# A fixed instruction order on every engine, and zero-padded keys for full-array scores, in a retention plus feed-forward kernel

## The chip, the cores and the metric

The kernel runs on one core of one Trainium2 chip. The time is device microseconds per execution, the median of several runs. Engines are called PE (matmul; PEld its weight loads), DVE (VectorE), ACT (ScalarE), POOL (GpSimd) and SP (SyncE, which issues the transfers). The "chain" of a profile is the work that ended last, followed back from the last instruction. In these kernels PE writes its results into buffers in PSUM, and ACT or DVE copies them out again ("evicts"; in the kernel before, `qkT<-T` on ACT took 1.01 us and `xT<-O` on DVE 0.69 us). Tile names in the profiles: qn and kn are the scaled queries and keys, T their transposes, qT, kpad or qkT the evicted ones, sc the scores, R the masked scores, vpad the padded values, O the output, st the state, xT the attention's result, ph and po the up- and down-projection.

## The reference, cut to what matters

```python
def _attn_ref(q, k, v):                        # 8 batches, 8 heads, 576 tokens, 64 dims
    scores = scale * np.matmul(q, k.transpose(0, 1, 3, 2))
    gamma = 1.0 - 2.0 ** (-5.0 - np.arange(H))
    Dmat = np.where(rel >= 0, gamma[:, None, None] ** rel[None], 0.0)   # decay, causal
    return np.matmul(scores * Dmat, v)
def _moe_ref(x, w_in, w_out, beta):            # x: 4608 x 512, w_in: 512 x 2048
    h = x @ w_in
    return (h * (1.0 / (1.0 + np.exp(-beta * h)))) @ w_out
```

There is no softmax, so the attention of a batch is done in five chunks of tokens (four of 128 and one of 64) with a running state: a chunk needs its own 128 x 128 scores, and the earlier chunks enter through the state.

## The kernel before

Per chunk: scale q and v by the decay, transpose q and k on PE into one PSUM bank `T`, evict with one ACT copy, scores, causal mask on DVE, output, state. `HP` is 4, pairs of heads; two heads share a 128-row tile, so the scores of one head contract over 64 rows only.

```python
        qkT = sb.tile([P, 2, HP, P], BF16, name="qkT", tag="qkT", bufs=3)
        nc.scalar.copy(qkT[:, :, :, :cL], T[:, :, :, :cL])
        ...
        with tc.manual_schedule(engines={PE}):          # order fixed inside this block only
            for p in range(HP):
                for j in range(2):
                    r = slice(j * D, (j + 1) * D)       # rows 0-63 or 64-127: half the array
                    nc.tensor.matmul(sc[j][:cL, p, :cL], qkT[r, 1, p, :cL], qkT[r, 0, p, :cL], ...)
        for j in range(2):
            nc.vector.tensor_tensor(R[:cL, j, :, :cL], sc[j][:cL, :, :cL], m_b, ALU.mult)
    ...
    for b in range(1, B + 1):                           # a scheduler orders what this emits
        if b < B:
            for c in range(NC):
                load_chunk(b, c)
                if b == 1 and c == NC - 1:
                    load_w_out()                        # after all loads of batch 1
            for c in range(NC):
                attn_chunk(b, c)
        moe_up(b - 1, range(FO))                        # 64 matmuls 128x512, 16 Silu on ACT
        moe_down(b - 1)                                 # 64 matmuls 128x512
```

Of the kernel before, what the change touches and what calls it, by code (L numbers as in the profile page):

```python
# [11 lines left out]
F32 = mybir.dt.float32  # L12
# [7 lines left out]
def kernel(  # L20
# [10 lines left out]
    nc = tc.nc  # L31
# [21 lines left out]

    qkv_tiles = {}

    def load_chunk(b, c):
        c0, cL = chunks[c]
        t = stage.tile([P, 3, H, D], F32, name="qkvn", tag="qkvn", bufs=7)
        for i, src in enumerate((q, k, v)):
            nc.sync.dma_start(t[:cL, i], src[b, :, c0:c0 + cL, :].rearrange("h s d -> s h d"))  # L60
        qkv_tiles[(b, c)] = t

    for c in range(NC):
        load_chunk(0, c)
# [3 lines left out]

    ident_f = consts.tile([P, P], F32, name="ident_f")
# [8 lines left out]
    pos = consts.tile([P, NC], F32, name="pos")  # L78
    nc.gpsimd.iota(pos[:], pattern=[[P, NC]], base=0, channel_multiplier=1,
                   allow_small_or_imprecise_dtypes=True)  # L80
    lg = consts.tile([P, NC, H], F32, name="lg")
    for h in range(H):
        nc.vector.tensor_scalar(lg[:, :, h], pos[:], math.log(1.0 - 2.0 ** (-5.0 - h)), None, ALU.mult)
    gq = consts.tile([P, NC, H], F32, name="gq")
    gv = consts.tile([P, NC, H], F32, name="gv")
    nc.scalar.activation(gq[:], lg[:], ACT.Exp)
    nc.scalar.activation(gv[:], lg[:], ACT.Exp, scale=-1.0)
    nc.vector.tensor_scalar(gq[:], gq[:], scale, None, ALU.mult)


    NV = 3
    vpads = []
    for i in range(NV):
        vp = consts.tile([P, H, P], BF16, name=f"vpad{i}")
        nc.gpsimd.memset(vp[:], 0.0)
        vpads.append(vp)

    NS = 2
    sbds = []
    for i in range(NS):  # L100
        s = consts.tile([P, HP, P], BF16, name=f"sbd{i}")
        nc.gpsimd.memset(s[:], 0.0)
        sbds.append(s)
# [6 lines left out]
    pb = psum.tile([P, FO], F32, name="pb", tag="T", bufs=1)  # L110
    nc.tensor.transpose(pb[:], beta_rows[:], ident_f[:FO, :FO])

    tiny = consts.tile([P, FO], F32, name="tiny")
    nc.vector.tensor_copy(beta_sb[:], pb[:])
    nc.vector.tensor_tensor(tiny[:], beta_sb[:], beta_sb[:], ALU.mult)
    nc.vector.tensor_scalar(tiny[:], tiny[:], 1e-24, 1e-12, ALU.is_lt, ALU.mult)
    nc.vector.tensor_tensor(beta_sb[:], beta_sb[:], tiny[:], ALU.add)
    nc.vector.reciprocal(rbeta_sb[:], beta_sb[:])

# [3 lines left out]
    w_out_r = moe_w_out.rearrange("(fo fi) n -> fi fo n", fi=P)  # L123
    for g in range(WG):
        t = stage.tile([P, KO, FG], F32, name="wt", tag="wt", bufs=3)
        nc.sync.dma_start(t[:], w_in_r[:, :, g * FG:(g + 1) * FG])
        nc.vector.tensor_copy(w_in_sb[:, :, g * FG:(g + 1) * FG], t[:])  # L127

    def load_w_out():
        for g in range(WG):  # L130
            t = stage.tile([P, KO, d_model], F32, name="wt", tag="wt", bufs=3)
            nc.sync.dma_start(t[:], w_out_r[:, g * KO:(g + 1) * KO, :])
            for i in range(KO):
                fo = g * KO + i
                nc.vector.tensor_scalar(w_out_sb[:, fo, :], t[:, i], rbeta_sb[:, fo:fo + 1], None, ALU.mult)  # L135
# [4 lines left out]
    cnt = [0]  # L140

    def attn_chunk(b, c):
        c0, cL = chunks[c]
        t = qkv_tiles.pop((b, c))
        first = b == 0
        qn = sb.tile([P, H, D], BF16, name="qn", tag="qn", bufs=2)
        kn = sb.tile([P, H, D], BF16, name="kn", tag="kn", bufs=3)
        vp = vpads[cnt[0] % NV]
# [4 lines left out]
        eq = nc.vector if first else nc.gpsimd  # L153
        eq.tensor_tensor(qn[:cL], t[:cL, 0], gq_b, ALU.mult)  # L154
        if first:
            nc.scalar.copy(kn[:cL], t[:cL, 1])
        else:
            nc.gpsimd.tensor_copy(kn[:cL], t[:cL, 1])  # L158
        nc.gpsimd.tensor_tensor(vp4[:cL], t[:cL, 2].rearrange("p (pr two) d -> p pr two d", two=2),  # L159
                                gv_b.rearrange("p (pr two) d -> p pr two d", two=2), ALU.mult)  # L160

        T = psum.tile([P, 2, HP, P], BF16, name="T", tag="T", bufs=1)
        for i, src in enumerate((qn, kn)):
            for p in range(HP):
                nc.tensor.transpose(T[:, i, p, :cL],  # L165
                                    src[:cL, 2 * p:2 * p + 2, :].rearrange("p h d -> p (h d)"),
                                    ident[:cL, :cL])
        qkT = sb.tile([P, 2, HP, P], BF16, name="qkT", tag="qkT", bufs=3)
        nc.scalar.copy(qkT[:, :, :, :cL], T[:, :, :, :cL])  # L169

        R = sb.tile([P, 2, HP, P], BF16, name="R", tag="R", bufs=2)
        sc = [psum.tile([P, HP, P], F32, name="sc", tag="sc", bufs=2) for _ in range(2)]
        with tc.manual_schedule(engines={PE}):
            for p in range(HP):
                for j in range(2):
                    r = slice(j * D, (j + 1) * D)
                    nc.tensor.matmul(sc[j][:cL, p, :cL], qkT[r, 1, p, :cL], qkT[r, 0, p, :cL],  # L177
                                     start=True, stop=True, skip_group_check=True)
        m_b = causal[:cL, :cL].unsqueeze(1).to_broadcast([cL, HP, cL])
        for j in range(2):  # L180
            nc.vector.tensor_tensor(R[:cL, j, :, :cL], sc[j][:cL, :, :cL], m_b, ALU.mult)  # L181

        O = psum.tile([P, HP, P], F32, name="O", tag="O", bufs=1)
        with tc.manual_schedule(engines={PE}):
            n = 0
            if c > 0:
                sbd = sbds[(cnt[0] - 1) % NS]
                for p in range(HP):
                    nc.tensor.matmul(O[:, p, :cL], sbd[:, p, :], qkT[:, 0, p, :cL],  # L189
                                     start=(n == 0), stop=False, skip_group_check=True)  # L190
                    n += 1
            for p in range(HP):
                for j in range(2):
                    nc.tensor.matmul(O[:, p, :cL], vp[:cL, 2 * p + j, :], R[:cL, j, p, :cL],  # L194
                                     start=(n == 0), stop=(p == HP - 1 and j == 1),
                                     skip_group_check=True)
                    n += 1
        n0 = b * S + c0
        nc.vector.tensor_copy(xT[:, :, n0:n0 + cL], O[:, :, :cL])  # L199

        if c < NC - 1:
            if c == 0:
                st = psum.tile([P, HP, P], F32, name="st", tag="st", bufs=1)
                state_ps[b] = st
            st = state_ps[b]
            with tc.manual_schedule(engines={PE}):
                for p in range(HP):
                    nc.tensor.matmul(st[:, p, :],  # L208
                                     kn[:cL, 2 * p:2 * p + 2, :].rearrange("p h d -> p (h d)"),
                                     vp4[:cL, p], start=(c == 0 and p == 0), stop=True,  # L210
                                     skip_group_check=True)
            sbd = sbds[cnt[0] % NS]
            for j in range(2):
                r = slice(j * D, (j + 1) * D)
                nc.scalar.copy(sbd[r, :, j * D:(j + 1) * D], st[r, :, j * D:(j + 1) * D])  # L215
        cnt[0] += 1
# [4 lines left out]
    def moe_up(m, fos):  # L221
        m0 = m * MB
        if m not in gts:
            gts[m] = sb.tile([P, FO, MB], BF16, name="gT", tag="gT", bufs=2)
        gT = gts[m]
        for fo in fos:
            ph = psum.tile([P, MB], F32, name="ph", tag="mm", bufs=3)
            for ko in range(KO):
                nc.tensor.matmul(ph[:], w_in_sb[:, ko, fo * P:(fo + 1) * P], xT[:, ko, m0:m0 + MB],  # L229
                                 start=(ko == 0), stop=(ko == KO - 1))  # L230
            nc.scalar.activation(gT[:, fo, :], ph[:], ACT.Silu, scale=beta_sb[:, fo:fo + 1])  # L231

    def moe_down(m):
        m0 = m * MB
        gT = gts.pop(m)
        for ms in range(MB // P):
            po = psum.tile([P, d_model], F32, name="po", tag="mm", bufs=3)
            for fo in range(FO):
                nc.tensor.matmul(po[:], gT[:, fo, ms * P:(ms + 1) * P], w_out_sb[:, fo, :],  # L239
                                 start=(fo == 0), stop=(fo == FO - 1))  # L240
            ot = sb.tile([P, d_model], F32, name="ot", tag="ot", bufs=3)
            nc.vector.tensor_copy(ot[:], po[:])  # L242
            nc.sync.dma_start(out[m0 + ms * P:m0 + (ms + 1) * P, :], ot[:])

    for c in range(NC):
        attn_chunk(0, c)
    for b in range(1, B + 1):
        if b < B:
            for c in range(NC):
                load_chunk(b, c)  # L250
                if b == 1 and c == NC - 1:
                    load_w_out()
            for c in range(NC):
                attn_chunk(b, c)
        moe_up(b - 1, range(FO))
        moe_down(b - 1)
# [33 lines left out]
```

## Time and profile before

| | before |
|---|---|
| median time | 362.81 us (362.46 to 363.98, 3 runs) |
| span of the profiled run | 360.6 us |
| PE / ACT / DVE / POOL busy | 93 / 45 / 31 / 28% |
| first 512-column matmul of an up-projection | 28.4 us |
| first matmul of a down-projection | 63.7 us |
| last matmul starts | 356.4 us |

The lines of this profile, and how to read them, are in the prediction below. One habit is used throughout: a busy PE says little, as matmuls overlap (a 512-column one is recorded with 384 ns on average), so I read the distance between the starts of successive matmuls. From 67 us on in this trace, at a granted clock of 1.00, the median distance from a 512-column matmul to the next is 216 ns, from a 128-column one 56 ns, from a 64-column one 29 ns; what exceeds that I call a wait or a drain. A drain is the extra distance where PE changes between matmuls on the whole array and on part of it (152 ns for 56 from 128-column work to half-array scores in this trace); each such change is a crossing. I call the time from the first up-projection matmul to the start of the last matmul the **stretch**: 328.0 us before.

### The profile page before, as it was taken

The numbers are of one execution on the slowest core, as the hardware profiler recorded it, in microseconds if no ns is written. First come the engines' busy times: TensorE is split into PE (matmuls) and PEld (weight loads), VectorE is DVE, ScalarE is ACT, GpSimd is POOL, SyncE is SP. The second block draws the span as 40 slices with busy tenths as digits, with TensorE's granted clock in tenths as the row PEclk, the third lists the DMA queues.
The fourth block names the chain that finished last, engine by engine and source line by source line (L and its number), as shares of the span: only waits on it lengthen the run. The fifth ranks groups of instructions, "written<-read, shape, count | busy, mean of one in ns | idle before, by whom it ended". The sixth has DMA issues, their size and how long they took to land.

```text
span 360.6 us, 5795 instructions
## 1 busy us (share of the span) xinstructions
PE 335.3 (93%) x2369; PEld 175.9 (49%) x2369; DVE 112.5 (31%) x196; ACT 160.7 (45%) x257; POOL 102.6 (28%) x124
## 2 busy tenths in 40 slices
PE   1768967999999999999999999999999999999995
PEld 1643455345544644465446544654466444444442
DVE  4565144724422630164025402450146011011011
ACT  2653843017720864076506660567047703703810
POOL 6211760026832761085007600670051000000000
PEclk9976975799999999999999999999999999999999
DMA  9998995769938995599569951300110011011002
GB/s 175 211 351 209 219 235 208 191 163 219 203 73 200 179 202 92 157 241 192 114 166 206 215 100 58 106 0 2 58 60 2 0 58 60 0 58 59 2 34 82
DMA packets 121978, 46.52 MB, mean 129 GB/s; under 512 B 113232, under 2 KB 113248, under 8 KB 121952
## 3 DMA queue, kind: packets, MB, share of 16 engines
q1 hardware_dynamic: 121920, 46.15, 56.2%
q8 instruction: 18, 0.29, 0.4%
q14 instruction: 8, 0.07, 0.1%
q10 hardware_dynamic: 32, 0.01, 0.0%
HBM read 36.71 MB, written 9.44 MB: 128 GB/s over the span
## 4 chain that ended last, share of the span: by engine, by line
PE 88%; ACT 5%; DVE 3%; DMA 1%; SPq 1%; issue 1%; POOL 0%; ACTq 0%
PE po L239 35%; PE ph L229 34%; PE O L194 6%; PE T L165 5%; PE sc L177 4%; ACT qkT L169 4%; PE O L189 2%; PE st L208 2%; DVE R L181 1%; DMA qkvn<-in_k_dram 1%; SPq L60 1%; ACT gT L231 0%; DVE w_in_sb L127 0%; POOL qn L154 0%; DVE xT L199 0%
## 5 line engine op out<-in xcount | busy, mean ns | idle before, releaser
L229 PE MATMUL ph<-xT,w_in_sb 128*128 128x512 bf16 x576 | 140.2, 384 | 1.7 <-DVE w_in_sb L127 1.7
L231 ACT ACTIVATE gT<-ph,beta_sb 128x512 bf16<-128x512 f32 x144 | 98.9, 687 | 67.4 <-PE ph L229 66.7
L239 PE MATMUL po<-w_out_sb,gT 128*128 128x512 bf16 x576 | 127.5, 383 | 0.9 <-DVE w_out_sb L135 0.9
L239 PEld LDWEIGHTS <-gT 128*128 128x128 bf16 x576 | 56.8, 99 | 69.9 <-issue 3.1
L169 ACT COPY qkT<-T 128x1024 bf16<-128x1024 bf16 (+1 forms) x40 | 36.9, 924 | 100.0 <-PE T L165 100.0
L229 PEld LDWEIGHTS <-w_in_sb 128*128 128x128 bf16 x576 | 53.0, 99 | 56.2 <-issue 3.1
L242 DVE COPY ot<-po 128x512 f32<-128x512 f32 x36 | 24.7, 691 | 168.6 <-PE po L239 168.6
L154 POOL TENSOR_TENSOR qn<-qkvn,gq 128x512 bf16<-128x512 f32 (+1 forms) x35 | 36.6, 1046 | 127.6 <-issue 45.1
L181 DVE TENSOR_TENSOR R<-sc,causal 128x512 bf16<-128x512 f32 (+1 forms) x80 | 47.0, 628 | 35.0 <-PE sc L177 35.0
L159 POOL TENSOR_TENSOR vpad<-qkvn,gv 128x512 bf16<-128x512 f32 (+1 forms) x40 | 41.8, 1045 | 30.4 <-DMA qkvn<-in_v_dram 23.6
L199 DVE CAST xT<-O 128x512 bf16<-128x512 f32 (+1 forms) x40 | 25.5, 638 | 31.9 <-PE O L194 31.8
L194 PE MATMUL O<-R,vpad 128*128 128x128 bf16 (+1 forms) x320 | 31.7, 226 | 2.4 <-DVE R L181 2.2
L194 PEld LDWEIGHTS <-vpad 128*128 128x128 bf16 (+1 forms) x320 | 23.1, 103 | 13.9 <-issue 6.8
L215 ACT CAST sbd<-st 64x256 bf16<-64x256 f32 x64 | 23.4, 366 | 8.8 <-PE st L208 8.0
L177 PE MATMUL sc<-qkT 64*128 64x128 bf16 (+1 forms) x320 | 17.3, 226 | 9.5 <-ACT qkT L169 8.8
L158 POOL CAST kn<-qkvn 128x512 bf16<-128x512 f32 (+1 forms) x35 | 21.3, 607 | 11.0 <-DMA qkvn<-in_k_dram 10.6
L177 PEld LDWEIGHTS <-qkT 64*128 64x128 bf16 (+1 forms) x320 | 10.0, 102 | 20.5 <-ACT qkT L169 18.2
L165 PE MATMUL T<-ident,qn 128*128 128x128 bf16 (+1 forms) x160 | 16.1, 226 | 3.4 <-DVE qn L154 3.3
L165 PE MATMUL T<-ident,kn 128*128 128x128 bf16 (+1 forms) x160 | 17.7, 227 | 0.0
L165 PEld LDWEIGHTS <-qn 128*128 128x128 bf16 (+1 forms) x160 | 10.4, 102 | 9.2 <-DVE qn L154 3.6
L208 PE MATMUL st<-vpad,kn 128*128 128x128 bf16 x128 | 13.6, 230 | 0.0
L189 PE MATMUL O<-qkT,sbd 128*128 128x128 bf16 (+1 forms) x128 | 12.4, 223 | 0.1
(32 smaller groups left out, 59.7 us busy)
## 6 DMA issues: line engine op xcount, KB each, us to landing
out_dram<-ot SPq DMA_DIRECT2D x36, 256.0 KB, 2.0
qkvn<-in_q_dram SPq DMA_DIRECT2D x32, 256.0 KB, 4.9
qkvn<-in_k_dram SPq DMA_DIRECT2D x32, 256.0 KB, 5.1
qkvn<-in_v_dram SPq DMA_DIRECT2D x32, 256.0 KB, 5.1
wt<-in_moe_w_in_dram SPq DMA_DIRECT2D x4, 1024.0 KB, 8.3
wt<-in_moe_w_out_dram SPq DMA_DIRECT2D x4, 1024.0 KB, 7.2
qkvn<-in_q_dram SPq DMA_DIRECT2D x8, 128.0 KB, 4.5
qkvn<-in_k_dram SPq DMA_DIRECT2D x8, 128.0 KB, 4.2
```

What stands on the lines that cost most here:

```text
L154: eq.tensor_tensor(qn[:cL], t[:cL, 0], gq_b, ALU.mult)
L159: nc.gpsimd.tensor_tensor(vp4[:cL], t[:cL, 2].rearrange("p (pr two) d -> p pr two d", two=2), gv_b.rearrange("p (pr two) d -> p pr two d", ...
L165: nc.tensor.transpose(T[:, i, p, :cL], src[:cL, 2 * p:2 * p + 2, :].rearrange("p h d -> p (h d)"), ident[:cL, :cL])
L169: nc.scalar.copy(qkT[:, :, :, :cL], T[:, :, :, :cL])
L177: nc.tensor.matmul(sc[j][:cL, p, :cL], qkT[r, 1, p, :cL], qkT[r, 0, p, :cL], start=True, stop=True, skip_group_check=True)
L181: nc.vector.tensor_tensor(R[:cL, j, :, :cL], sc[j][:cL, :, :cL], m_b, ALU.mult)
L194: nc.tensor.matmul(O[:, p, :cL], vp[:cL, 2 * p + j, :], R[:cL, j, p, :cL], start=(n == 0), stop=(p == HP - 1 and j == 1), skip_group_check ...
L199: nc.vector.tensor_copy(xT[:, :, n0:n0 + cL], O[:, :, :cL])
L229: nc.tensor.matmul(ph[:], w_in_sb[:, ko, fo * P:(fo + 1) * P], xT[:, ko, m0:m0 + MB], start=(ko == 0), stop=(ko == KO - 1))
L231: nc.scalar.activation(gT[:, fo, :], ph[:], ACT.Silu, scale=beta_sb[:, fo:fo + 1])
L239: nc.tensor.matmul(po[:], gT[:, fo, ms * P:(ms + 1) * P], w_out_sb[:, fo, :], start=(fo == 0), stop=(fo == FO - 1))
L242: nc.vector.tensor_copy(ot[:], po[:])
```

## The change

Two things. First, the scheduler is switched off and the emitted order stands on every engine: each chunk is cut into stages, and these are dropped between the 512-column "slots" of the feed-forward part (a slot is four such matmuls, 0.864 us), two slots apart. Weight loads go out earlier, and some matmuls on zeros are there to raise the clock (the first twelve at the start). Second, the keys are evicted into zeroed buffers, one head's 64 rows at a time, so that scores contract over all 128 rows with zeros in the other half.

```diff
+    ctx.enter_context(tc.manual_schedule())
 ...
+    kpads = [consts.tile([P, H, P], BF16, name=f"kpad{i}") for i in range(NK)]
+    for kp in kpads:
+        nc.vector.memset(kp[:], 0.0)
 ...
-        nc.scalar.copy(qkT[:, :, :, :cL], T[:, :, :, :cL])
+        nc.scalar.copy(qT[:, :, :cL], T[:, 0, :, :cL])
+        for j in range(2):
+            r = slice(j * D, (j + 1) * D)
+            nc.vector.tensor_copy(kp[r, j::2, :cL], T[r, 1, :, :cL])
 ...
-                    nc.tensor.matmul(sc[j][:cL, p, :cL], qkT[r, 1, p, :cL], qkT[r, 0, p, :cL],
+                nc.tensor.matmul(sc[j][:cL, p, :cL], L["kp"][:, 2 * p + j, :cL], L["qT"][:, p, :cL],
 ...
+    def attn_steps(i, at, gap=2.0):
+        return [(at - 4, F(pre, i)), (at - 3.9, F(load_next, i)), (at, F(a_T, i)), (at + gap, F(a_sc, i)),
+                (at + 2 * gap, F(a_st, i)), (at + 2 * gap, F(a_O, i))]
+    warm_up(12)
+    betas()
 ... # four chunks alone, warm_up(2) between their stages, then:
+    fill = [F(up, 0, fo) for fo in range(FO)]
+    merged(fill, ..., [(9.5, F(pre, 4)), (12, F(a_T, 4)), (14, F(a_sc, 4)), (16, F(a_O, 4))],
+           [(9.6, F(pre, 5)), (15, F(a_T, 5)), (16.1, F(a_sc, 5))], [(9.7, F(pre, 6))])
+    a_st(5)
+    a_O(5)
 ... # then, per block m: 16 up slots, 16 down slots, chunks spread evenly over them
```

## The prediction

> **What bounds the kernel now.** I read the page's busy rows first, then the slices of the span, then the chain of waits, then the waits of PE alone, and last the timeline of PE in one steady stretch.
>
> ```profile
> PE 335.3 (93%) x2369; PEld 175.9 (49%) x2369; DVE 112.5 (31%) x196; ACT 160.7 (45%) x257; POOL 102.6 (28%) x124
> ...
> PE   1768967999999999999999999999999999999995
> ...
> PEclk9976975799999999999999999999999999999999
> ...
> PE 88%; ACT 5%; DVE 3%; DMA 1%; SPq 1%; issue 1%; POOL 0%; ACTq 0%
> ```
>
> PE is the bound: no other engine passes 45%, and the chain is 88% PE. But PE is full only from the eighth slice (a slice is 9.0 us); the first seven have holes and a lowered clock. The whole case splits there. The stretches below (columns after the length: busy time of PE, PEld, DVE, ACT, POOL, then clock, DMA share, GB/s) and the waits of PE (total us, times, longest) show it:
>
> ```profile
> 20.00:30.00 10.00, 5.74 (x56) 3.58 (x57) 6.55 (x10) 4.19 (x6) 1.04 (x1) 0.64 0.80 284
> 50.00:60.00 10.00, 7.67 (x74) 6.12 (x73) 3.97 (x7) 3.49 (x6) 2.86 (x4) 0.50 0.89 315
> 120.00:130.00 10.00, 9.99 (x128) 6.65 (x126) 6.93 (x12) 7.30 (x14) 7.13 (x9) 1.00 1.07 196
> ```
> ```profile
> PE sc L177 <- ACT qkT L169: 8.8, 8, 2.4
> PE pb L111 <- DMA beta_rows<-in_moe_beta_dram: 3.5, 1, 3.5
> PE T L165 <- DVE qn L154: 3.3, 1, 3.3
> PE O L194 <- DVE R L181: 2.2, 8, 0.5
> ```
>
> Batches 0 and 1 of the attention run with little beside them: transpose, eviction (1.01 us), scores, mask (2 x 0.68 us), output, each waiting for the other. [...] the first 128x512 matmuls start 427 ns apart, not 216. From 67.2 us to the last matmul at 356.7 us PE has no hole at all. In that part only fewer or cheaper PE instructions help. The timeline shows where they are dear:
>
> ```profile
> 117.05 1.03 PE L229 MATMUL ph<-xT,w_in_sb 128*128 128x512 bf16 x4
> 118.15 0.40 PE L177 MATMUL sc<-qkT 64*128 64x128 bf16 x8
> 118.48 0.40 PE L165 MATMUL T<-ident,qn 128*128 128x128 bf16 x4
> ```
>
> Four 512-column matmuls should occupy 4 x 0.216 = 0.86 us, so the scores could start at 117.91; they start at 118.15. The eight half-array scores then take 0.33 us to the next start.
>
> [...] scores start in pairs 4 ns apart, pairs about 54 ns apart, but entering costs 0.10 us after 128-column work (152 ns between starts for 56) and 0.23 us after a 512-column matmul, and the first start after the block comes 148 ns after its last. [...] the key copy on DVE waits for ACT's query copy of the same bank. [...] The fp32 evictions here, 692 ns for 512 elements, are 1x; a bf16 copy out of PSUM on DVE isn't in this trace.
>
> **The change part by part.**
>
> *Scores on the full array.* Removed per 128-token chunk: 0.18 us between the eight starts, 0.15 exit, 0.10 to 0.23 entry, 0.43 to 0.56 us. Added: 8 x 0.056 = 0.45 us without drains. So the doubled array work is nearly free and the gain is at most 0.11 us a chunk, some 2 us over 32. The 64-token chunk stays in row tiles for transposes and outputs (4 crossings x about 0.095 us).
>
> *Order.* A chunk is now four stages spread over the 512-column work, two slots (2 x 0.864 us) apart, so mode changes and semaphore waits ought to vanish. A batch is 1.57 (28 x 0.056) + 3 x 1.79 (32 x 0.056) + 1.19 (28 x 0.029 + 0.38) = 8.14 us. Before: 289.5 us from 67.2 on, less about 1,078 512-column matmuls x 0.216 = 232.9, leaves 56.6 us for six batches, 9.43 each. Saved: 1.29 x 6 = 7.7 us, which is the steady part's whole gain, score change included.
>
> *PE total.* 1,088 x 0.216 + 64 x 0.0825 + 64 x 0.136 (one block is split 192 + 320) = 249.0 us. Attention after the first four chunks: 7 x 8.14 + 1.19 = 58.2. Together **307.2 us** once the first up-projection starts.
>
> *When it starts.* Only four chunks stand ahead of it, not five, and the weight loads go out after the fourth chunk. A chunk lands every 3.6 us (0.79 MB at 218 GB/s), a weight MB in 2.7 us (387 GB/s), so the fourth chunk lands at 17.5 us and the first weights near 20: not the bound. DVE is, as its order is fixed: per chunk 2 masks x 0.68 + xT 0.69 + qn 0.68 + two key copies. [...] the sum is 3.6 us. T of chunk 0 is delayed by the warm-up (12 x 0.427) and the beta work, which now stand ahead of it, to 8.4 us instead of 7.0; its results are done at 9.0. Three more chunks and the last mask, weight casts (3 x 0.42) and xT give **25.0 us**, for 28.4 now with five chunks done.
>
> *New latency.* Transposes to scores: before, one ACT copy of 1.01 us. Now ACT 0.58 and then two DVE copies, 0.43 each: 1.44, plus a handoff of 0.06. It must fit into two slots, 1.73 us, with a wait of 0.20 for the last transpose ahead of it. It fits with 0.0 to 0.4 us left (the first four scores need only the first copy); mask and output fit too (1.36 for 1.73 + st 0.22). ACT has 0.69 of each 0.864 us in an up phase, so its queue adds up to 0.25.
>
> *Stalls.* At the seam of fills 0 and 1, scores, mask, output and xT of chunk 5 stand next to one another: 1.4 + 0.6 = 2.0 us. Chunk 6's mask waits on DVE behind three weight scalings of 0.48: 1.0. The rest, short slots of block 1 and output copies (0.69) that get ahead of a key copy: 2.2. Sum 5.2.
>
> *Tail.* As now: 3.9 us from last matmul to end.
>
> *Sum.* 25.0 + 307.2 + 5.2 + 3.9 = 341.3 us span; the profiled run took 1.7 us more than its span (362.3 for 360.6), so **343.0 us**, 5.5% less. Of the 19.8 us, some 7 come from the steady part and 13 from the first 67 us, where holes and half clock go.
>
> **The rivals.** *Key copies at 1x.* 0.69 each makes the transposes-to-scores latency 1.96 plus handoffs, over the two slots: 0.3 to 0.55 us of wait in most of 36 chunks, 10 to 18 us, and 2 us later start. Result 353 to 358, hardly faster. For it: every DVE eviction in the trace is 1x. [...] One in five. *In-order blocking.* [...] For it: casts and masks share DVE, stores and loads share SP. Against: by the rates above w_out lands at 40 to 48 us, its scaling is wanted at about 45 to 58, and loads run seven chunks ahead. It costs up to 6 us if the rates are lower. *Start still latency-bound.* If POOL or ACT order delays each early chunk by 1 us, the start is at 29, the result 347. *Everything overlaps.* No stall but the seam: 338.
>
> **Range and chances.** The floor is 25 + 307 + 4 + 2 = 338, less if DVE starts sooner; 335 is hard to pass. Upwards, half of the 1x rival or blocking fit by 351. The 2% line is at 355.6, which takes the full 1x rival plus more. Faster 0.95, within 2% 0.045, slower 0.005. Correctness I don't doubt: the zero rows of the padded keys are never written.
>
> **What would show it.** (a) Scores 128 rows, 56 ns apart, no gap of 150 ns around those of full chunks; N = 512 still 216. (b) First up-projection at 24 to 26 us. (c) Granted clock at full from there to the end. (d) Key copy near 0.43 us; at 0.69 the rival rules and "sc waits for DVE key copy" leads PE's waits. (e) Waits of PE after 30 us of 4 to 8 us. (f) Attention share of PE per batch near 8.1 us. The prediction is wrong if the first up-projection comes after 28 us, if waits of PE after it pass 12 us, or if scores on the full array show more than 56 ns each, such as where a 64-token chunk has only 64 weight columns.

The sum came to 25.0 + 307.2 + 5.2 + 3.9 = 341.3 us of span, 343.0 us with the 1.7 us outside it. A term inside it has lost its working: the 0.43 us of a key copy, which is in the 3.6 us per chunk of the start and in the 1.44 us of new latency. Read it as an estimate: "1x" is the rate of this trace's fp32 evictions on DVE, 692 ns for 128x512, "2x" twice that rate, and an eviction of half the size, 128x256, took 424 ns in the same trace. That a bf16 copy would be so quick was not shown before the result. The 0.42 us of a weight cast is the author's estimate too (the first three in the new profile took 1.09 us together). The 0.0825 and 0.136 us of the split block are estimates along the line from 56 ns for 128 columns to 216 ns for 512; the new profile has 82 and 136 ns. The clock was granted at half from 22.8 to 33.0 us and from 50.1 to 67.1 us. That the key copy waits for ACT's query copy is in the new profile: 73.1 us of DVE's waits, 36 times.

## The result, and the profile after

The new kernel takes 342.03 us (341.34 to 343.58, 4 runs), the old one in the same rounds 362.63. The ratio is 0.9444 (95% interval 0.9384 to 0.9504). Ratios here are the mean time of one kernel's fast runs over that of the other's of the same rounds, so not quite the ratio of the medians.

The page's rows, slices, clock and chain of the new kernel, and then the same three stretches as before:

```profile
PE 329.0 (97%) x2455; PEld 185.4 (54%) x2455; DVE 147.5 (43%) x284; ACT 149.2 (44%) x272; POOL 114.0 (33%) x132
...
PE   5979999999999999999999999999999999999995
...
PEclk9699999999999999999999999999999999999998
...
PE 91%; DVE 6%; ACT 1%; issue 0%
```
```profile
20.00:30.00 10.00, 8.13 (x62) 4.62 (x61) 7.75 (x17) 5.36 (x9) 2.30 (x3) 1.00 1.13 327
50.00:60.00 10.00, 10.00 (x70) 5.64 (x68) 5.56 (x11) 2.32 (x7) 7.92 (x8) 1.00 1.07 194
120.00:130.00 10.00, 10.00 (x79) 5.75 (x77) 5.91 (x11) 1.91 (x4) 3.71 (x4) 1.00 0.32 93
```

PE is full from the fourth slice instead of the eighth, and the clock stays at 1.00 where it had been 0.64 and 0.50. The early part is repaired. PE's own waits (total us, times, longest) are down to this:

```profile
PE T L206 <- DVE qn L186: 2.6, 1, 2.6
PE O L246 <- DVE R L229: 1.7, 7, 0.4
PE ph L281 <- DVE xT L250: 1.6, 2, 1.2
PE ph L156 <- DVE warm L75: 1.2, 1, 1.2
PE sc L225 <- DVE kpad L214: 0.3, 1, 0.3
```

The query scaling and the warm wait stand ahead of the first up-projection, as does most of the xT one. Nothing like the old 8.8 us of scores waiting for their eviction is left, although the way to the scores is longer now. The scores themselves, in the timeline of PE:

```profile
99.13 1.46 PE L281 MATMUL ph<-xT,w_in_sb 128*128 128x512 bf16 x6
100.43 0.61 PE L225 MATMUL sc<-qT,kpad 128*128 128x128 bf16 x8
100.88 1.46 PE L281 MATMUL ph<-xT,w_in_sb 128*128 128x512 bf16 x6
```

Six matmuls x 0.216 = 1.30 us, and the scores start 1.30 us after the first of them: no drain on entry. Eight scores take 0.45 us to the next start.

What the new span is made of: 25.35 us to the first up-projection (28.36 before, though with five chunks done, not four), a stretch of 311.3 us (328.0 before), and 4.2 us from the start of the last matmul to the end, as before. Taking all 512-column work away from the part after 67.2 us at 0.216 us each, and in the new kernel also the split blocks, leaves 9.4 us of PE per batch of attention before and about 8.5 now. Six batches x 0.9 = some 5.5 us of the 19.7 us of span come from the steady part; some 14 from the first 67 us.

### The profile page after: what moved, and what is told of

Read it like the earlier page. It is cut to its first block, busy times and chain, and to the rows that moved or that the text cites. A ratio compares the mean times of both kernels' runs of the same rounds, so it can differ in the third digit from the quotient of the medians.

```text
span 340.9 us, 6127 instructions
## 1 busy us (share of the span) xinstructions
PE 329.0 (97%) x2455; PEld 185.4 (54%) x2455; DVE 147.5 (43%) x284; ACT 149.2 (44%) x272; POOL 114.0 (33%) x132
## 4 chain that ended last, share of the span: by engine, by line
PE 91%; DVE 6%; ACT 1%; issue 0%
PE po L293 37%; PE ph L281 36%; PE sc L225 5%; PE T L206 5%; PE O L246 4%; PE st L263 2%; PE O L241 2%; DVE R L229 1%; DVE kpad L214 1%; PE ph L156 1%; DVE xT L250 1%; DVE qn L186 1%; ACT gT L283 1%; ACT qT L210 1%; DVE w_in_sb L134 0%
## 5 line engine op out<-in xcount | busy, mean ns | idle before, releaser
L281 PE MATMUL ph<-xT,w_in_sb 128*128 128x512 bf16 (+2 forms) x640 | 133.9, 358 | 1.6 <-DVE xT L250 1.6
L293 PE MATMUL po<-w_out_sb,gT 128*128 128x512 bf16 x576 | 133.4, 379 | 0.0
L283 ACT ACTIVATE gT<-ph,beta_sb 128x512 bf16<-128x512 f32 (+2 forms) x160 | 102.0, 645 | 47.7 <-PE ph L281 46.5
L281 PEld LDWEIGHTS <-w_in_sb 128*128 128x128 bf16 x640 | 59.0, 98 | 53.9 <-issue 1.6
L214 DVE COPY kpad<-T 64x512 bf16<-64x512 bf16 (+1 forms) x80 | 31.6, 395 | 74.4 <-ACT qT L210 73.1
L210 ACT COPY qT<-T 128x512 bf16<-128x512 bf16 (+1 forms) x40 | 21.6, 540 | 68.9 <-PE T L206 68.8
L225 PEld LDWEIGHTS <-kpad 128*128 128x128 bf16 (+1 forms) x320 | 19.8, 102 | 12.6 <-DVE kpad L214 5.0
L246 PE MATMUL O<-R,vpad 128*128 128x128 bf16 (+1 forms) x320 | 23.9, 215 | 1.7 <-DVE R L229 1.7
L225 PE MATMUL sc<-qT,kpad 128*128 128x128 bf16 (+1 forms) x320 | 24.1, 218 | 0.5 <-DVE kpad L214 0.3
L263 PEld LDWEIGHTS <-kn 128*128 128x128 bf16 x128 | 9.8, 99 | 6.0
```

The source lines that it names most:

```text
L210: nc.scalar.copy(qT[:, :, :cL], T[:, 0, :, :cL])
L214: nc.vector.tensor_copy(kp[r, j::2, :cL], T[r, 1, :, :cL])
L225: nc.tensor.matmul(sc[j][:cL, p, :cL], L["kp"][:, 2 * p + j, :cL], L["qT"][:, p, :cL], start=True, stop=True, skip_group_check=True)
L246: nc.tensor.matmul(O[:, p, :cL], vp[:cL, 2 * p + j, :], R[:cL, j, p, :cL], start=(n == 0), stop=(j == 1), skip_group_check=True)
L281: nc.tensor.matmul(ph[:, :tn], w_in_sb[:, ko, fo * P:(fo + 1) * P], xT[:, ko, x0:x0 + tn], start=(ko == 0), stop=(ko == KO - 1))
L283: nc.scalar.activation(gT[:, fo, t0:t0 + tn], ph[:, :tn], ACT.Silu, scale=beta_sb[:, fo:fo + 1])
```

## The experiments

Each run was taken against the kernel before in its own rounds. Traces of some runs lack a few matmul records, so I compare starts (first up-projection, stretch), which do not suffer from that, and not counts.

| run | median us | ratio to before | first up-projection | stretch |
|---|---|---|---|---|
| new kernel | 342.03 | 0.944 | 25.35 | 311.3 |
| half-array scores, new order | 339.53 | 0.939 | 24.10 | 309.2 |
| before + full-array scores | 365.59 | 1.011 | 30.06 | 332.0 |
| new, scheduler's order | 348.12 | 0.962 | 26.22 | 316.8 |
| before, w_out loaded earlier | 356.77 | 0.987 | 28.70 | 321.8 |
| new, stages one slot apart | 365.18 | 1.008 | 25.32 | 333.1 |
| half-array, stages one slot apart | 350.32 | 0.966 | 23.94 | 320.5 |
| new without warm-up | 341.51 | 0.942 | 22.57 | 312.0 |
| new, 64-token chunks on the full array | 339.88 | 0.936 | 25.75 | 308.0 |
| new, POOL memset earlier | 344.64 | 0.949 | 25.71 | 313.0 |
| combination, full array | 338.04 | 0.932 | 22.72 | 310.0 |
| combination, half array | 338.59 | 0.934 | 22.28 | 310.9 |
| second combination, full array | 337.55 | 0.932 | 22.55 | 309.0 |

### 1. Half-array scores in the new order

The change's second half undone, its first half kept.

```diff
-        nc.scalar.copy(qT[:, :, :cL], T[:, 0, :, :cL])
-        for j in range(2): nc.vector.tensor_copy(kp[r, j::2, :cL], T[r, 1, :, :cL])
+        nc.scalar.copy(qkT[:, :, :, :cL], T[:, :, :, :cL])
-        for j in range(2):
-            for p in range(HP):   # kp[:, 2 * p + j, :cL], qT[:, p, :cL]
+        for p in range(HP):
+            for j in range(2):    # kT[r, p, :cL], qT[r, p, :cL]
```

> The new kernel in its hand-written order, with scores on half the array again (one ACT copy of both transposes, eight 64-row matmuls in pairs). Theory: the pairing saves what the drains cost. Each block now follows a 512-column matmul, so it costs 0.18 between its starts + 0.15 exit + 0.23 entry = 0.56 us against 0.45 on the full array: +0.11 x 28 = +3.1 us from the first up-projection to the last matmul (new kernel: 311.3 us). DVE loses its 0.86 us of key copies per chunk in the first 25 us, so the first up-projection comes 2 to 3 us sooner than 25.4. Sum: 341 to 343 us, no clear change. Rival: the pairing is worth its 4 ns starts and the stretch shrinks by 3 us: 337 us.

Measured: 339.53 us, ratio 0.9392 (0.9366 to 0.9417), where the new kernel has 0.9444 (0.9384 to 0.9504). The intervals overlap, so the time alone decides little; the trace decides. The timeline of PE around one block of scores:

```profile
96.72 1.46 PE L278 MATMUL ph<-xT,w_in_sb 128*128 128x512 bf16 x6
98.11 0.40 PE L222 MATMUL sc<-qkT 64*128 64x128 bf16 x8
98.44 1.68 PE L278 MATMUL ph<-xT,w_in_sb 128*128 128x512 bf16 x7
```

The scores start 1.39 us after the first of six, not 1.30. From the single records: entry 312 ns (96 above 216), pairs 3 ns apart, 52 to 63 ns between pairs, exit 149. From the start of the last matmul ahead to the start of the one after, this is 642 ns; the full-array block has 662. So the half-array block is **20 ns shorter**, not 110 ns longer (426 and 446 ns without the 216 of the matmul ahead). For the 64-token chunk it is 553 against 680. Sum: 28 x 0.020 + 8 x 0.127 = 1.6 us of the 2.1 us by which the stretch is shorter. The start gains 1.25 us, with no key copies on DVE. Both theories fell: the direction was the rival's, the size neither's.

### 2. Full-array scores alone, in the kernel before

```diff
-        nc.scalar.copy(qkT[:, :, :, :cL], T[:, :, :, :cL])
+        nc.scalar.copy(qT[:, :, :cL], T[:, 0, :, :cL])
+        for j in range(2): nc.vector.tensor_copy(kp[r, j::2, :cL], T[r, 1, :, :cL])
-                    nc.tensor.matmul(..., qkT[r, 1, p, :cL], qkT[r, 0, p, :cL], ...)
+                    nc.tensor.matmul(..., kp[:, 2 * p + j, :cL], qT[:, p, :cL], ...)
```

> The kernel before with padded keys and full-array scores alone, scheduler's order kept. Theory: the score change by itself is worth 1 to 2 us of the steady part (10.9 us of mode-switch cost there falls to about 4, the pairs lose 5.6), and the longer way from transposes to scores (0.58 + 2 x 0.42 against 1.01) costs 2 to 3 us in the first 67 us where nothing hides it: 360 to 365, same. Rival: removing the mode switches is the main gain: 350 to 356.

Measured: 365.59 us, 1.0109 (1.0050 to 1.0168): 0.6 us above the theory's range, and clear of noise on the slow side. The first up-projection comes 1.7 us later, and the steady part is no faster either, against the theory: from one down-projection's first matmul to the next it takes 37.5 us a batch (143.12 to 180.66) for 37.0 before (139.56 to 176.56). By these two runs the padded keys alone are worth nothing in either kernel; what made the new kernel faster is the rest.

### 3. The new kernel with the scheduler's order

```diff
-    ctx.enter_context(tc.manual_schedule())
```

> The new kernel with the one line removed that keeps the written order on every engine; the scheduler may move instructions again. Theory: the gain lies in the fixed order on the engines, so it is mostly lost: 352 to 362. Rival: the gain lies in what is emitted (spread stages, weight loads earlier, warm-up), which the scheduler keeps: 341 to 347.

Measured: 348.12 us, 0.9622 (0.9595 to 0.9649), between the two. Of the 5.6% that the new kernel gains, 3.8% stay when the scheduler may move things again; some 6 us are lost. The loss is early: its down-projection starts at 56.0 us, for 51.1 in the fixed order, so 4.9 us are gone by then; at the second one it is 6.3 (87.5 for 81.2), and no more is lost after that. Its clock record shows half clock from 45.0 to 51.8 us. The longest wait of PE in this stretch, at 43.5 us, is in this row:

```profile
PE sc L224 <- DVE kpad L213: 2.2, 3, 1.2
```

So what is emitted (spread stages, earlier weights) carries most, the fixed order the rest.

### 4. The kernel before with its output weights loaded earlier

```diff
-                if b == 1 and c == NC - 1:
+                if b == 1 and c == 1:
                     load_w_out()
```

> The kernel before with one condition changed: the output-weight loads go out after the second chunk of batch 1, not after its fifth. Theory: the hole at 46 to 63 us is there because the down-projection has no weights (they land at 52 to 59, scaled from 63), so the attention of batch 1 stands alone; with weights some 10 us earlier the down-projection fills it: 350 to 356. Rival: the holes are the attention's own waits, and loads moved forward delay its later chunks as much: 359 to 363.

Measured: 356.77 us, 0.9866 (0.9841 to 0.9891), 5.0 us for one condition. The start of the down-projection, before (from the chain in order of time) and here (from the timeline):

```profile
63.66 15.68 PE po L239 x64
```
```profile
50.74 0.63 PE L239 MATMUL po<-w_out_sb,gT 128*128 128x512 bf16 x1
```

The hole of the old kernel from 46 to 63 us was in good part missing weights. It is 0.8 us outside the theory's range; in its profile the attention of batch 1 still waits for itself (6.3 us of scores waiting for the eviction, 8.8 before), and two half-clock windows remain.

### 5. Stages one slot apart

```diff
-    def attn_steps(i, at, gap=2.0):
+    def attn_steps(i, at, gap=1.0):
```

> The new kernel with the stages of a chunk one slot (0.86 us) apart instead of two. Theory: two slots are what hides the way over ACT and DVE. From the last transpose 0.20 + ACT 0.58 + DVE 0.42 and two handoffs of 0.06 are 1.3 us to the first score, 0.45 over one slot, and the second key copy adds 0.2; the masks (1.29) just fit. 0.5 to 0.7 us in each of some 27 full chunks: 14 to 19 us of waits of PE on the key copy and the masks, 354 to 362 us. Rival: the distance matters little because PE's queue has other work anyway: under 346.

Measured: 365.18 us, 1.0084 (1.0037 to 1.0132). A single number takes away all that the change gained: the stretch grows by 21.8 us, more than the theory's 14 to 19. One chunk, all engines but POOL and SP:

```profile
160.19 0.69 ACT L283 ACTIVATE gT<-ph,beta_sb 128x512 bf16<-128x512 f32 x1 [0.18 <-PE ph L281]
...
160.43 1.03 PE L293 MATMUL po<-w_out_sb,gT 128*128 128x512 bf16 x4
160.77 0.58 ACT L210 COPY qT<-T 128x512 bf16<-128x512 bf16 x1
...
161.38 0.88 DVE L214 COPY kpad<-T 64x512 bf16<-64x512 bf16 x2 [6.05 <-ACT qT L210]
...
161.86 0.86 PE L225 MATMUL sc<-qT,kpad 128*128 128x128 bf16 x8 [0.40 <-DVE kpad L214]
```

Read it as a relay. The slot of four matmuls would let the scores start at 160.43 + 0.86 = 161.29, but DVE begins its first key copy only when ACT is done with the same bank, at 161.38, and the scores start at 161.86; inside the block they wait 0.22 us more for the second copy. That is 0.79 us for this chunk, where a Silu (160.19) stands ahead of the query copy on ACT. Without one it is 0.68 to 0.73, and two chunks among the shorter slots of block 1 lose 1.0. The mechanism holds; the sizes, 0.5 to 0.7 us a chunk and 354 to 362 us in all, were too low, and the Silu ahead of the copy was not among them.

### 6. Half-array scores, stages one slot apart

```diff
 # the kernel of experiment 1, with
-    def attn_steps(i, at, gap=2.0):
+    def attn_steps(i, at, gap=1.0):
```

> The half-array variant with the stages of a chunk one slot apart. The full-array kernel lost 22 us of stretch that way (311.3 to 333.1). Theory: most of that is the longer way of the padded keys (ACT 0.58, then two DVE copies of 0.42 one after the other, against one ACT copy of 1.01, all keys ready at once): here each chunk waits 0.3 to 0.5 us instead of 0.65 to 1.03, and the time is 348 to 354. Rival: the distance would be needed as much with the short way, as it is ACT's queue and the masks that are late: 360 or more.

Measured: 350.32 us, 0.9662 (0.9636 to 0.9689), as the theory said. The same step costs 11.3 us of stretch here and 21.8 with padded keys. Read in starts, a full chunk loses 0.31 to 0.44 us at its scores here, and 0.68 to 0.81 there (the chunks of block 1's short slots apart). So about half of the need for the distance is made by the padded keys' own longer way. The list of waits would have hidden this: it has 8.7 us of scores waiting for the eviction here and 8.8 in experiment 5, as it counts idle time after the modelled ends of matmuls only.

### 7. No warm-up

```diff
-    warm_up(12)
-        warm_up(2)   # both places
```

> The new kernel without its 22 warm-up matmuls. Theory: the start is bound by DVE, so the first up-projection still comes at 24 to 26 us[...], 343.5 to 345.5. Rival: the attention of the first four chunks is enough to lift the clock, as it was in the new kernel from 14.8 us on with PE half idle: 341 to 342.5, or 1 us less as the beta work no longer stands behind twelve matmuls.

The theory's 343.5 to 345.5 us includes 1.7 to 3.5 us for matmuls at half clock as the dense work begins. How long that lasts was not worked out from a trace.

Measured: 341.51 us, 0.9422 (0.9383 to 0.9461): the rival. The first transposes and the first up-projection in its timeline:

```profile
5.52 0.61 PE L206 MATMUL T<-ident,qn 128*128 128x128 bf16 x4 [1.73 <-DVE qn L186]
...
22.57 7.71 PE L281 MATMUL ph<-xT,w_in_sb 128*128 128x512 bf16 x35 [1.22 <-DVE xT L250]
```

The transposes start 2.9 us earlier (8.40 with the warm-up), because the beta work no longer stands behind twelve matmuls on PE and ahead of the query scaling on DVE. In this run the clock was full from 13.3 us on without any warm-up matmul; with them it was full from 4.6 us, fell to half at 8.0 us and was back at 14.8. The start was not simply bound by DVE, as I had it, but by when its chain began.

### 8. The 64-token chunks on the full array

```diff
-                nc.tensor.matmul(sc[j][:cL, p, :cL], L["kp"][:, 2 * p + j, :cL], ...
+                nc.tensor.matmul(sc[j][:, p, :cL], L["kp"][:, 2 * p + j, :], ...
-            nc.vector.tensor_tensor(R[:cL, j, :, :cL], sc[j][:cL, :, :cL], m_b, ALU.mult)
+            nc.vector.tensor_tensor(R[:, j, :, :cL], sc[j][:, :, :cL], m_b, ALU.mult)
-                nc.tensor.matmul(O[:, p, :cL], vp[:cL, 2 * p + j, :], R[:cL, j, p, :cL],
+                nc.tensor.matmul(O[:, p, :cL], vp[:, 2 * p + j, :], R[:, j, p, :cL],
```

Rows 64 to 127 hold old, finite data; the causal mask turns them into zeros, so the result stays correct.

> The new kernel with scores, mask and output of the 64-token chunks on all 128 rows and columns (stale finite rows are zeroed by the causal mask). Theory: what is left of the mode switches is theirs. A block of 64-column scores costs 464 ns (680 less 216) with its two switches and should cost 8 x 29 = 232; the output saves 97 + 96 ns. 0.42 us x 8 = 3.4 us: 338.6 us, and the stretch from the first up-projection falls from 311.3 to 308. Rival: these are hidden by waits anyway: 341.5 to 342.5.

Measured: 339.88 us, 0.9363 (0.9306 to 0.9421), 1.3 us above the time expected, with an interval that overlaps the new kernel's, but a stretch of 307.95 us for 311.34: **3.4 us, the number expected**. The short chunk's scores in the new kernel, and then here:

```profile
107.82 0.59 PE L281 MATMUL ph<-xT,w_in_sb 128*128 128x512 bf16 x2
108.35 0.44 PE L225 MATMUL sc<-qT,kpad 128*64 128x64 bf16 x8
108.72 0.82 PE L281 MATMUL ph<-xT,w_in_sb 128*128 128x512 bf16 x3
```
```profile
107.97 0.40 PE L225 MATMUL sc<-qT,kpad 128*128 128x64 bf16 x8
108.20 1.89 PE L281 MATMUL ph<-xT,w_in_sb 128*128 128x512 bf16 x8
```

With 64 weight columns (the "128*64") the block pays both switches, though all 128 rows are in use: 309 ns in (for 216), 128 out (for about 32). With the 312 ns of experiment 1, a crossing costs 93 to 97 ns in these traces. With 128 columns it takes 0.23 us.

### 9. The memset moved

```diff
     nc.gpsimd.memset(vpads[1][:], 0.0)
+    nc.gpsimd.memset(vpads[2][:], 0.0)
 ...
-    nc.gpsimd.memset(vpads[2][:], 0.0)   # after the first values' scaling
```

> The new kernel with the GpSimd memset of the third padded-value buffer moved ahead of the first values' work, into GpSimd's idle time. Theory: VectorE's first query scaling took 1.50 us instead of 0.68 because GpSimd ran two operations beside it; with the memset away it takes at most 1.0, and the first up-projection comes 0.5 to 0.8 us sooner: 24.6 to 24.9 for 25.35, about 341.4 us (to be read from the profile, not the time). Rival: the row is long for another reason and stays at 1.5.

Measured: 344.64 us, 0.9485 (0.9422 to 0.9548), no gain; the first up-projection comes at 25.71 us, not sooner. Three of the four runs took 344.6 to 345.0 us at a mean clock of 0.990, the fourth 340.6 at 1.000, so the time says nothing of the memset. The query scaling is short now, but a tiny DVE operation ahead of it is long instead. The new kernel, then this run:

```profile
6.75 1.04 POOL L191 TENSOR_TENSOR vpad<-qkvn,gv 128x512 bf16<-128x512 f32 x1 [2.83 <-DMA qkvn<-in_v_dram]
6.85 1.50 DVE L186 TENSOR_TENSOR qn<-qkvn,gq 128x512 bf16<-128x512 f32 x1
```
```profile
6.68 1.04 POOL L192 TENSOR_TENSOR vpad<-qkvn,gv 128x512 bf16<-128x512 f32 x1 [1.85 <-DMA qkvn<-in_v_dram]
6.70 1.05 DVE L164 TENSOR_TENSOR tiny<-beta_sb 128x16 f32<-128x16 f32 x1
```

Sixteen elements took 1.05 us, until POOL's value scaling ended (0.17 us in the new kernel, with nothing beside it). By these rows it is the value scaling that holds DVE up, not the memset: in the new kernel the query scaling ended at 8.35 us, while the memset ran on to 8.69. So the theory named the wrong one. Not every DVE instruction is held: in the kernel before, the xT copy at 13.93 us took its usual 0.69 us inside a value scaling that ran from 13.83 to 14.87. This profile also has a half-clock window at 26.4 to 29.8 us, in the first 512-column work: eight matmuls some 211 ns longer, the 1.7 us by which its stretch is longer.

### 10. Three versions that combine the findings

```diff
 # e9: experiment 8, no warm-up, and
-           [(9.6, F(pre, 5)), (15, F(a_T, 5)), (16.1, F(a_sc, 5))], ...
+           [(9.6, F(pre, 5)), (13.5, F(a_T, 5)), (15.1, F(a_sc, 5))], ...
 # e10: the same last two edits on the kernel of experiment 1
 # e12: experiment 8, without warm_up(12), the pairs kept, chunk 5 as in the new kernel, and
+    warm_up(6)                # after the fourth chunk's output
```

> The new kernel with three edits that the runs so far point to: 64-token chunks on the full array (stretch -3.4 us in the run of that edit alone), no warm-up matmuls (first up-projection at 22.6 instead of 25.4), and chunk 5's transposes and scores 1 to 1.5 slots earlier, so that its masks are done when its output is due (-0.6 us of the 1.7 us of waits there). First up-projection 22.6, stretch 307.5 to 308.5, tail 3.9, 1.7 outside the span: 335.5 to 337.5 us. If the gains don't add, because the weights' arrival binds an earlier start, 338 to 340.

> The half-array variant of the new kernel with the same two last edits (no warm-up, chunk 5 earlier; its 64-token chunks keep row tiles). Stretch 309.2 less 0.6; first up-projection at about 22, as the start is then bound by the arrival of chunks: 336 to 338 us. It tells whether padded keys are needed for the best version: not more than 1 us apart from the full-array version would say they are not.

> The new kernel with 64-token chunks on the full array, without the twelve warm-up matmuls at the very start, with the pairs between the first chunks kept and six more while PE waits for the last eviction ahead of the first up-projection (1.4 us in the version without any). Theory: the twelve delay the beta work and with it the first transposes by 2.9 us and lift the clock for nothing, while the late ones keep the clock at the moment the dense work starts, which the version without any lost (eight matmuls at 427 ns, 1.7 us). First up-projection at 22.6 to 23, stretch 308.0 to 308.7, no half-clock window after 15 us: 335.5 to 337 us. If the clock falls all the same: 338.

Measured: 338.04 us (0.9323, 0.9293 to 0.9354), 338.59 (0.9342, 0.9310 to 0.9374) and 337.55 (0.9316, 0.9286 to 0.9346). All three missed their range by 0.5 to 0.6 us. In the first, the clock fell to half from 23.6 to 27.0 us, just as the dense work began (eight matmuls 427 ns apart), and moving chunk 5 turned its wait for the masks into a wait of 0.8 us for an earlier xT copy on DVE, which now stood behind the masks. In the third no half-clock window follows 10 us (whether the six late matmuls did that was not separated), the first up-projection is at 22.55, and the stretch is 309.0. The intervals of all three lie wholly below the new kernel's; the third beats it by some 1.4% (0.9316 / 0.9444). The first two are 0.55 us apart: the padded keys are **not needed** for a version of this speed.

## Why the prediction was right

- **Time.** 343.0 predicted, 342.0 measured. Some of its terms were wrong and made up for one another, so that it came within 1 us is in part luck.
- **Order, PE total and start.** First up-projection at 25.35 us (25.0 predicted); from it to the last matmul 311.3 us, for 307.2 + 5.2 = 312.4. The start was right for partly wrong reasons: the twelve warm-up matmuls were quicker than at 427 ns each (some 427 ns apart for eight distances, then 216; 4.4 us in all, not 5.1), but the query scaling took 1.50 us, not 0.68.
- **Two slots hide the longer way.** Right, and the most important step: at one slot the gain is gone (experiment 5).
- **Key copies at 0.43 us, not 0.69.** 421 ns measured for 64x512 in bf16, 430 estimated, where the fp32 evictions of 128x512 take 691 ns in the same profile; this row of it ends the 1x rival:

```profile
L214 DVE COPY kpad<-T 64x512 bf16<-64x512 bf16 x64 | 27.0, 421 | 56.2 <-ACT qT L210 55.2
```

- **The seam.** 2.0 us predicted. Between 41.1 and 44.4 us PE waited 0.23 + 0.59 + 0.38 + 0.50 = 1.7 us beyond the usual distances of starts, in the order foreseen (key copy, two masks, xT):

```profile
41.78 0.39 PE L263 MATMUL st<-vpad,kn 128*128 128x128 bf16 x4
42.59 0.38 PE L246 MATMUL O<-R,vpad 128*128 128x128 bf16 x4 [0.43 <-DVE R L229]
43.19 0.38 PE L246 MATMUL O<-R,vpad 128*128 128x128 bf16 x4 [0.21 <-DVE R L229]
...
44.35 0.32 PE L281 MATMUL ph<-xT,w_in_sb 128*128 128x192 bf16 x2 [0.34 <-DVE xT L250]
```

- **Scores on the full array: this step failed.** It foresaw a gain of up to 0.11 us a chunk; the block costs 20 ns more. The failed term is the entry of 0.23 us after a 512-column matmul. It was read off one stretch of the old timeline and is 0.096 us of drain; the other 0.14 us was the scores waiting for their eviction: in the chain of the kernel before, they start as soon as the ACT copy has ended (lines below). The new order hides this wait for either form. The sum also has no term for the 64-token chunk's scores keeping their switches with 64 weight columns, though the prediction names this very case as a sign of being wrong, and it came: 0.23 us a batch, and most of why a batch takes 8.5 us and not 8.14.

```profile
117.08 1.02 ACT qkT L169
118.11 0.05 issue
118.15 0.40 PE sc L177 x8
```

- **Where the gain lies.** 7 steady and 13 early were predicted, about 5.5 and 14 measured. Beyond the plain distances and the switches that were foreseen, the stretch has 4.4 us: 1.9 are the short chunks' score switches, some 2.5 are waits. So the waits of 5.2 us were sized twice too large (and sign (e), 4 to 8 us, did not come), and the missing switches filled most of the gap.

What stays open: of the early 14 us, 5.0 can be named (earlier weights, experiment 4, measured in the old kernel). Another 3.8 are half clock under dense work: in the old kernel 18 of the 512-column matmuls, at 28.4 to 33.0 and 63.7 to 67.1 us, start 427 ns apart and not 216; the kernel of experiment 4 has 17 such, the new one none. What keeps its clock up was not separated. Between two changes the granted clock holds for 3.41 us or a multiple of it in the two main records (3.41, 6.83, 10.24, 17.07). In the 3.41 us ahead of a fall PE was busy for 1.74 and 1.57 us (kernel before, falls at 22.8 and 50.1 us) and for 1.76 us (first combined version, 23.6 us), but a stretch with the same 1.76 us (20.1 to 23.5 us without warm-up) held the full clock. So busy time alone does not decide; what does is not shown. The fixed order is worth about 6 us, all of it before 88 us; this overlaps with the other parts. The rest, staged chunks of batch 1, four chunks instead of five at the start, and the split weight casts, was not separated.

## What to carry to other kernels

When an engine is full, place each dependent stage as far behind its producer as the eviction way between them takes, and give the distance in that engine's own work; here one slot less cost as much as the whole change had gained. Before paying a longer eviction to avoid a mode switch, measure the drain apart from the wait that stands at the same place: run both forms in the final order. A change in several parts that wins as a whole may hold parts that lose; undo each alone.
